# A later slot for one remainder step, matmuls on zeros before the first attention units, and decay tables computed behind the casts

## The chip, the core and the metric

The kernel runs on one core of a Trainium2 chip. The metric is the device time of the launch in microseconds (us); the median of several runs is given. The core's engines are TensorE (PE in the profile, its weight loads PEld), VectorE (DVE), ScalarE (ACT), GpSimd (POOL) and SyncE (SP). DMA is issued here from SP and from POOL.

## The reference, cut to what matters

Two stages follow each other. The first is a decayed attention without softmax over 8 batches, 8 heads, 576 positions and 64 dimensions of a head; the second is a mixture of 4 experts with given weights.

```python
scores = (1 / sqrt(64)) * (q @ k.T)                 # per batch and head, 576 x 576
D = where(i >= j, gamma[h] ** (i - j), 0)           # gamma[h] = 1 - 2 ** (-5 - h)
attn = (scores * D) @ v                             # (8, 8, 576, 64)

x = attn.transpose(0, 2, 1, 3).reshape(4608, 512)
p = probs / (probs.sum(-1) + 1e-9)                  # (4608, 4)
out = sum(p[:, e] * (relu(x @ w1[e]) @ w2[e]) for e in range(4))   # w1 512x1024, w2 1024x512
```

## The kernel before, in words

The decay is split: keys are multiplied by a table `gk` that grows with their position, and the results by a table `gq` that falls with the query's position, so that only a triangular 0/1 mask stays between them. Attention is done in chunks of 128 positions. Inside a chunk scores are masked and multiplied with v; earlier chunks come in as a running sum of k times v (`sbd`). A batch has 576 positions, four chunks and a remainder of 64 positions, which the class `Rem` handles for all heads at once.

The second stage works on 9 tiles of 512 tokens. A tile goes through 4 experts: four up groups (`up_group`, 8 matmuls of 128x128 by 512 each, with the ReLU) and then, in tile 0, two down groups (`down_plain`, 16 such matmuls each). That makes 24 slots, 0 to 23. In slots 0 to 3, 6 to 9, 12 to 15 and 18 to 21 an up group runs, in the others a down group. Later tiles have another form of the down product and 30 slots.

Everything else is hung into these slots by hand. `slots` maps a slot number to a list of functions; `run(slots, n)` calls them right after the matmuls of slot n, in the order in which they were added. Each engine then executes its share in program order. So a slot number sets at the same time the place in TensorE's order, in VectorE's, in ScalarE's and in SP's queue.

Before tile 0 come the four units of batch 0 (class `Unit`; a unit is half of the four chunks for four heads). A unit's `cast` scales k on VectorE, converts q on ScalarE and v on GpSimd. Its `trans_pe` transposes k and q on TensorE and copies them out, q with ScalarE and k with VectorE. Then come `scores`, `kv` and `values`. These steps are interleaved by hand in the loop at lines 587 to 596. The result goes to the tile `xt`, the input of the up groups. The four rows of the table `gq` are computed on ScalarE ahead of all this (line 157), as is the exponential of `gk0`.

In tile 0 these steps hang in slots:

- `remainder(slots, 0, (-1, 11, 15, 16))`: in slot 11 the casts of the remainder of batch 0 and two transposes by DMA from SP (`kTr`, `qTr`, line 299); in slot 15 its scores (`sr`, line 305); in slot 16 its values (`or`, lines 311 and 313). The input `rawr` was loaded from GpSimd's queue.
- The four units of batch 1, with (cast, scores, values) at (14, 18, 19), (17, 21, 22), (21, 24, 26) and (24, 28, 30), counted on into tile 1. Their transposes (line 491) are DMAs from SP.
- `load_p(1, e, nc.sync)` in slot 17: four DMAs of 256 KB each from SP that spread the mixing weights of tile 1 over the partitions (`pB`).
- `w_sum` in slots 17 to 26: sums of weights on VectorE, for the down product of later tiles.

The weights of the experts are loaded with a conversion from GpSimd's queue (`load_w1` line 100, `load_w2` line 103), in the order w1 of expert 0, w2 of 0, w1 of 1, w2 of 1, w1 of 2, the remainder's inputs, w2 of 2, inputs of batch 1's first unit, w1 of 3, inputs of its second unit, w2 of 3. PSUM is a ring of four tiles (`ring_tile`) that all products share.

Of the kernel before, what the change touches and what calls it, by code (L numbers as in the profile page):

```python
# [10 lines left out]
BF16 = mybir.dt.bfloat16  # L11
# [12 lines left out]
def kernel(  # L24
# [10 lines left out]
    nc = tc.nc  # L35
    B, H, S, D = q.shape
    N, E = moe_domain_probs.shape
    _, Dm, F = moe_w1.shape
# [6 lines left out]
    NP = H // 2  # L45
# [20 lines left out]
    def ring_tile(name, shape, dt=FP32):  # L66
        return ring.tile(shape, dt, tag="ring", name=name)
# [11 lines left out]
    def load_rem(b, eng=nc.sync):  # L79
        for j in range(2):  # L80
            for n, src in (("k", k), ("v", v)):
                eng.dma_start(out=rawr[n][64 * j:64 * j + 64, :, j, :],  # L82
                                  in_=src[b, j:H:2, SM:S, :].rearrange("g t d -> t g d"))
        eng.dma_start(out=rawr["q"][0:R, :, :, :].rearrange("t g j d -> t (g j) d"),
                          in_=q[b, :, SM:S, :].rearrange("h t d -> t h d"))
# [13 lines left out]
    def load_w1(e):  # L99
        return nc.gpsimd.dma_start(out=w1_sb[e], in_=moe_w1[e].rearrange("(dc p) f -> p dc f", p=128))  # L100
# [7 lines left out]
    epool = early.enter_context(tc.tile_pool(name="epool", bufs=1))  # L108
# [18 lines left out]
    nc.sync.dma_start(out=prb, in_=moe_domain_probs.rearrange("(p t) e -> p t e", p=128))  # L127


    pos_0 = epool.tile([128, 2, 2], FP32)  # L130
    nc.gpsimd.iota(pos_0, pattern=[[2 * C, 2], [1, 2]], base=0, channel_multiplier=2,
                   allow_small_or_imprecise_dtypes=True)
# [20 lines left out]
    lsc = epool.tile([128, 1], FP32)  # L153
    nc.vector.memset(lsc, math.log(scale))
    gq = const.tile([128, NP, S], FP32)
    for p in range(NP):
        nc.scalar.activation(gq[:, p, :], pos_i, Exp, scale=lgp[:, p:p + 1], bias=lsc)  # L157

    tri = const.tile([128, C], BF16)
# [49 lines left out]
    def load_p(t, e, eng):  # L209
        pB[t, e] = ppool.tile([128, NT], FP32, tag="pB", name="pB")  # L210
        eng.dma_start(out=pB[t, e], in_=pd[e:e + 1, t * NT:(t + 1) * NT].to_broadcast([128, NT]))  # L211
# [369 lines left out]

    bfv0 = lambda g: {(n, hf): bf0[n][:, hf, g] for n in "kqv" for hf in range(2)}
    us = [Unit(0, hf, g, raw0[u], bfv0(g)) for u, (hf, g) in enumerate(units0)]
    us[0].cast(nc.gpsimd)
    us[0].trans_pe()
    us[1].cast(nc.gpsimd)
    for u in range(NU):
        us[u].scores()
        us[u].kv()
        if u + 1 < NU:  # L590
            us[u + 1].trans_pe()
        if u == 0:
            load_w1(0)
        if u + 2 < NU:
            us[u + 2].cast(nc.gpsimd)
        us[u].values()
# [51 lines left out]
    def remainder(slots, b, at):  # L648
        add = lambda i, f: slots.setdefault(i, []).append(f)
        x = Rem(b)  # L650
        l, c, s, o = at
        if b > 0:
            add(l, lambda: load_rem(b))
        add(c, x.cast)
        add(c, x.trans_dma)
        add(s, x.scores)
        add(o, x.values)
# [4 lines left out]

    slots = {}
    add = lambda i, f: slots.setdefault(i, []).append(f)
    remainder(slots, 0, (-1, 11, 15, 16))

    def v_cast(u):
        vs[u].cast()
        vs[u].trans_dma()
        if u == 0:  # L670
            load_v(2, nc.gpsimd)
        elif u == 2:
            load_v(3, nc.gpsimd)
        elif u == 3:
            load_pair(raw1, 2, 0)

    def v_head(u):
        vs[u].scores()
        vs[u].kv()

    for u, (c, sc, o) in enumerate(((14, 18, 19), (17, 21, 22), (21, 24 + 0, 24 + 2), (24 + 0, 24 + 4, 24 + 6))):
        add(c, lambda u=u: v_cast(u))
        add(sc, lambda u=u: v_head(u))
        add(o, lambda u=u: vs[u].values())
    add(17, lambda: [load_p(1, e, nc.sync) for e in range(E)])
    for j in range(4):
        for wi, which in enumerate((3, 1, 2, 4)):
            add((17, 19, 22, 25)[j] + wi // 2, lambda which=which, j=j: w_sum(which, 4 * j, 4 * j + 4))
# [1 line left out]
    n = 0  # L690
# [11 lines left out]
    for t in range(1, n_nt):  # L702
        slots = {i - 24: f for i, f in slots.items() if i >= 24} if t == 1 else {}
# [6 lines left out]
        add = lambda i, f: slots.setdefault(i, []).append(f)  # L710
# [12 lines left out]
        n = 0  # L723
# [43 lines left out]
```

## Time and profile before

| what | value |
|---|---|
| median of 8 runs | 559.71 us |
| lowest and highest of them | 557.65 and 562.08 us |
| the profiled execution's own time | 560.53 us |
| its span in the trace | 558.7 us |
| PE busy in the span | 538.4 us (96%) |
| DVE busy | 375.5 us (67%) |
| ACT busy | 110.8 us (20%) |
| POOL busy | 55.0 us (10%) |
| bytes moved by DMA | 64.28 MB, mean 115 GB/s |

The profile's page cuts the span into 40 slices of 14 us each and gives a digit for the busy share of each engine in a slice. A row PEclk gives the granted TensorE clock in tenths of full speed. The view of stages gives the same for any stretch of the span. The timeline lists instructions with start, duration, and in brackets how long the engine had been idle and what ended the wait. The chain of work that ended last names, from the last instruction back, what released each step. The busy time of PE contains modelled ends of matmuls, so a PE that is shown busy need not run at its peak.

### The profile page before, as it was taken

Reading aid. Unit: us, or ns where it says so; the run is one execution under the profiler, and the core shown is the slowest. Engines: PE = TensorE matmul, PEld = TensorE weight load, DVE = VectorE, ACT = ScalarE, POOL = GpSimd, SP = SyncE. Lnnn points to the kernel's source line nnn. Section 1 sums busy time; section 2 is a strip of 40 time slices with the busy share of each in tenths; the row PEclk is TensorE's granted clock in tenths of the full one; section 3 lists DMA queues with packets and bytes.
Section 4 is the critical chain, followed back from the end, with each engine's and each line's share of the span. In section 5 each row is a group of like instructions: output and inputs, shape, how many; then the busy total and the mean of one; then the engine's idle time right before and its main releaser. Section 6 shows DMA issues by size and latency. Waiting matters only on the chain.

```text
span 558.7 us, 10556 instructions
## 1 busy us (share of the span) xinstructions
PE 538.4 (96%) x4416; PEld 351.7 (63%) x4416; DVE 375.5 (67%) x550; ACT 110.8 (20%) x216; POOL 55.0 (10%) x95
## 2 busy tenths in 40 slices
PE   4999599999999999999999999999999999999996
PEld 3544245888854686468645874588447854884485
DVE  4622067988668874897389838984788567736871
ACT  5323313303211220122013201131113100000010
POOL 4613101010000000000000000000000000000000
PEclk9999899999999999999999999999999999999999
DMA  9999918557635752577145824753367131010010
GB/s 238 165 205 238 224 34 217 103 100 152 170 91 122 151 143 72 122 133 171 57 113 131 148 87 95 156 125 103 91 136 146 51 97 40 21 57 19 1 39 38
DMA packets 147454, 64.28 MB, mean 115 GB/s; under 512 B 127216, under 2 KB 137584, under 8 KB 147408
## 3 DMA queue, kind: packets, MB, share of 16 engines
q1 hardware_dynamic: 137760, 44.35, 34.9%
q0 software_dynamic: 9648, 19.27, 16.1%
q8 instruction: 34, 0.56, 0.4%
q14 instruction: 12, 0.10, 0.1%
HBM read 53.56 MB, written 9.51 MB: 113 GB/s over the span
## 4 chain that ended last, share of the span: by engine, by line
PE 92%; DMA 3%; DVE 2%; ACT 1%; issue 1%; SPq 1%; POOL 0%; POOLq 0%; DVEq 0%; ACTq 0%
PE ph L326 37%; PE pd L429 35%; PE po L359 5%; PE ph L344 5%; DMA qTr<-bfr_q 2%; PE kvp L246 2%; PE o L270 1%; PE s L259 1%; PE o L273 1%; PE kvp L525 1%; DMA rawr_q<-in_q_dram 1%; PE pt L483 1%; PE s L506 1%; ACT gq L157 1%; SPq L82 0%
## 5 line engine op out<-in xcount | busy, mean ns | idle before, releaser
L326 PE MATMUL ph<-xt,w 128*128 128x512 bf16 x1024 | 228.8, 382 | 0.0
L326 PEld LDWEIGHTS <-w 128*128 128x128 bf16 x1024 | 99.3, 99 | 115.4 <-issue 2.9
L332 DVE SCALAR_TENSOR_TENSOR h<-ph,pB 128x1024 bf16<-128x1024 f32 x112 | 136.2, 1222 | 31.9 <-PE ph L326 31.6
L429 PEld LDWEIGHTS <-h 128*128 128x128 bf16 x1024 | 98.7, 98 | 12.2
L429 PEld LDWEIGHTS <-s 128*128 128x128 bf16 x768 | 74.3, 98 | 8.9
L429 PE MATMUL pd<-wx,h 128*128 128x256 bf16 x512 | 61.2, 273 | 0.0
L429 PE MATMUL pd<-wx,s 128*128 128x256 bf16 x512 | 61.1, 273 | 0.0
L251 ACT ACTIVATE sbd<-kvp 64x256 bf16<-64x256 f32 x48 | 18.1, 378 | 111.1 <-PE kvp L246 110.8
L261 DVE TENSOR_TENSOR sT<-s,tri 128x1024 bf16<-128x1024 f32 x24 | 29.2, 1217 | 10.9 <-PE s L259 10.9
L211 POOL DMA_DIRECT2D pB<-pd x28 | 15.2, 542 | 206.9 <-DVE h L332 168.5
L455 POOL TENSOR_TENSOR ob<-v,p 128x256 f32<-128x256 f32 x16 | 11.6, 724 | 231.5 <-DVE v L452 139.0
L359 PE MATMUL po<-wx,h 128*128 128x512 bf16 x128 | 31.0, 401 | 0.0
L429 PE MATMUL pd<-t4w,h 128*128 128x256 bf16 x256 | 30.6, 273 | 0.0
L429 PE MATMUL pd<-t2w,s 128*128 128x256 bf16 x256 | 30.6, 273 | 0.0
L446 DVE TENSOR_TENSOR u<-pd,p 128x256 f32<-128x256 f32 x16 | 6.8, 422 | 35.4 <-issue 29.5
L429 PE MATMUL pd<-t3w,h 128*128 128x256 bf16 x256 | 30.6, 273 | 0.0
L344 PE MATMUL ph<-xt,w 128*128 128x256 bf16 x256 | 29.2, 273 | 0.2 <-DVE h L347 0.2
L280 DVE TENSOR_TENSOR xt<-o,gq 128x384 bf16<-128x384 f32 (+6 forms) x48 | 18.0, 416 | 16.0 <-PE o L273 16.0
L344 PEld LDWEIGHTS <-w 128*128 128x128 bf16 x256 | 24.7, 98 | 3.2
L437 ACT ACTIVATE p<-pd 128x256 f32<-128x256 f32 x16 | 6.1, 383 | 95.5 <-PE pd L429 73.8
L330 ACT ACTIVATE h<-ph 128x1024 bf16<-128x1024 f32 x16 | 16.4, 1023 | 40.6 <-PE ph L326 40.6
L408 DVE TENSOR_TENSOR h<-h 128x1024 bf16<-128x1024 bf16 x32 | 23.4, 770 | 0.0
(130 smaller groups left out, 418.5 us busy)
## 6 DMA issues: line engine op xcount, KB each, us to landing
pB<-pd POOLq DMA_DIRECT2D x28, 256.0 KB, 3.7
raw_k<-in_k_dram SPq DMA_DIRECT2D x48, 128.0 KB, 2.9
raw_q<-in_q_dram SPq DMA_DIRECT2D x48, 128.0 KB, 3.3
raw_v<-in_v_dram SPq DMA_DIRECT2D x48, 128.0 KB, 3.4
w<-in_moe_w_dram POOLq DMA_DIRECT2D x4, 1024.0 KB, 13.1
wx<-in_moe_w_dram POOLq DMA_DIRECT2D x4, 1024.0 KB, 17.2
out_dram<-oa SPq DMA_DIRECT2D x16, 256.0 KB, 2.0
out_dram<-ob SPq DMA_DIRECT2D x16, 256.0 KB, 2.0
```

Source lines behind the costliest of these rows:

```text
L211: eng.dma_start(out=pB[t, e], in_=pd[e:e + 1, t * NT:(t + 1) * NT].to_broadcast([128, NT]))
L251: nc.scalar.activation(sbd[r, self.p, :, r], kvp[r, :, :], Copy)
L261: nc.vector.tensor_tensor(self.sT[:, :, :, :].rearrange("p j c t -> p (j c) t"), s[:, :, :, :].rearrange("p j c t -> p (j c) t"), tri[:, : ...
L280: nc.vector.tensor_tensor(xt_of(t)[:, p, n0 + a - t * NT:n0 + z - t * NT], o[:, a:z], gq[:, p, a:z], op=MULT)
L326: nc.tensor.matmul(ph[:, f, :], lhsT=w1_sb[e][:, dc, fc * 128:(fc + 1) * 128], rhs=x[:, dc, :], start=(dc == 0), stop=(dc == NDC - 1))
L330: nc.scalar.activation(h[:, fk:fk + 2, :], ph, Relu)
L332: nc.vector.scalar_tensor_tensor(h[:, fk:fk + 2, :], ph, 0.0, pB[t, e][:, :].unsqueeze(1).to_broadcast([128, 2, NT]), op0=MAX, op1=MULT)
L344: nc.tensor.matmul(ph[:, f, :], lhsT=w1_sb[e][:, dc, fc * 128:(fc + 1) * 128], rhs=x[:, dc, c], start=(dc == 0), stop=(dc == NDC - 1))
L359: nc.tensor.matmul(po[:, g, :], lhsT=h[:, e * NFC + fc, ns * 128:(ns + 1) * 128], rhs=wx[e // 2][:, (e % 2) * NFC + fc, :, :].rearrange("p ...
L408: nc.vector.tensor_tensor(h[:, l, self.b], h[:, l, self.a], h[:, l, self.b], op=SUB)
L429: mm = nc.tensor.matmul(dst, lhsT=src[:, kk, tok], rhs=rhs(c), start=(start and c == 0), stop=(c == KH - 1), skip_group_check=True)
L455: nc.gpsimd.tensor_tensor(self.ob[:, HF:Dm], self.v, self.p5, op=ADD)
```

## The change

Three things change. First, the remainder of batch 0 in tile 0 is cast in slot 12 rather than 11, has its scores in slot 18 rather than 15 and its values in slot 19 rather than 16; to go with it the first unit of batch 1 has its scores in slot 19 rather than 18 and its values in slot 20 rather than 19, and the four loads of `pB` for tile 1 stand in slot 15 rather than 17. Second, eight matmuls on a tile of zeros (128x128 by 512) run on TensorE ahead of the first unit's transposes and three more behind them; the tile is filled by VectorE. Third, the rows of `gq` are no longer computed on ScalarE ahead of the first cast: rows 0 and 1 follow the first unit's `trans_pe`, rows 2 and 3 follow the first unit's `kv`. As the loop is written, that puts rows 2 and 3 ahead of the second unit's `trans_pe` in ScalarE's order.

```diff
+    zz = epool.tile([128, 512], BF16)
+    nc.vector.memset(zz, 0.0)
+
+    def warm(n):
+        w = ring_tile("w", [128, 512])
+        for _ in range(n):
+            nc.tensor.matmul(w, lhsT=zz[:, 0:128], rhs=zz, start=True, stop=True)
+
     pos_0 = epool.tile([128, 2, 2], FP32)
...
     gq = const.tile([128, NP, S], FP32)
-    for p in range(NP):
+
+    def make_gq(p):
         nc.scalar.activation(gq[:, p, :], pos_i, Exp, scale=lgp[:, p:p + 1], bias=lsc)
...
+    warm(8)
     us[0].cast(nc.gpsimd)
     us[0].trans_pe()
+    warm(3)
+    make_gq(0)
+    make_gq(1)
     us[1].cast(nc.gpsimd)
     for u in range(NU):
         us[u].scores()
         us[u].kv()
+        if u == 0:
+            make_gq(2)
+            make_gq(3)
         if u + 1 < NU:
             us[u + 1].trans_pe()
...
-    remainder(slots, 0, (-1, 11, 15, 16))
+    remainder(slots, 0, (-1, 12, 18, 19))
...
-    for u, (c, sc, o) in enumerate(((14, 18, 19), (17, 21, 22), (21, 24 + 0, 24 + 2), (24 + 0, 24 + 4, 24 + 6))):
+    for u, (c, sc, o) in enumerate(((14, 19, 20), (17, 21, 22), (21, 24 + 0, 24 + 2), (24 + 0, 24 + 4, 24 + 6))):
...
-    add(17, lambda: [load_p(1, e, nc.sync) for e in range(E)])
+    add(15, lambda: [load_p(1, e, nc.sync) for e in range(E)])
```

## The prediction

> **What bounds the kernel now.** I read the page's rows by slices first, then the stages around the slice that sticks out, then the timeline there and the chain of waits, and last the units ahead of tile 0. TensorE is at 9 everywhere but in the first slice and the last one, and in slices 3 and 4:
>
> ```profile
> PE   4999599999999999999999999999999999999996
> PEclk9999899999999999999999999999999999999999
> ```
>
> A PE digit of 5 and a clock digit of 8, both in slice 4 (56 to 70 us), mark one place where TensorE stood still and was slowed afterwards. The view of stages by 2 us (columns: PE busy, PEld, DVE, ACT, POOL, granted clock, DMA share, GB/s):
>
> ```profile
> 58.00:60.00 2.00, 2.00 (x10) 0.70 (x8) 0.00 (x0) 1.67 (x3) 0.00 (x0) 1.00 1.13 229
> 60.00:62.00 2.00, 0.02 (x1) 0.00 (x0) 0.00 (x0) 2.00 (x4) 1.49 (x2) 1.00 1.22 196
> 64.00:66.00 2.00, 0.00 (x0) 0.00 (x0) 0.00 (x0) 0.00 (x0) 0.00 (x0) 0.78 1.22 228
> 68.00:70.00 2.00, 2.00 (x6) 0.69 (x5) 0.00 (x0) 0.00 (x0) 0.00 (x0) 0.50 1.35 123
> 70.00:72.00 2.00, 2.00 (x6) 0.73 (x5) 0.00 (x0) 0.00 (x0) 0.00 (x0) 0.51 0.22 9
> 72.00:74.00 2.00, 2.00 (x17) 1.02 (x16) 0.85 (x2) 0.00 (x0) 0.00 (x0) 1.00 0.00 0
> ```
>
> No matmul runs from 60 to 66.9 us; the clock falls to half at 65.2 us (finer stages) and is back at 71.9. The DMA engines are full until 70 and empty from 71. The timeline says what TensorE waited for:
>
> ```profile
> 55.19 1.30 SPq L299 DMA_TRANSPOSE kTr<-bfr_k  x1
> 56.59 1.19 SPq L299 DMA_TRANSPOSE qTr<-bfr_q  x1
> 57.88 1.21 SPq L491 DMA_TRANSPOSE qkT<-bf_k  x1
> 59.90 2.10 SPq L491 DMA_TRANSPOSE qkT<-bf_q  x1
> ...
> 66.93 0.37 PE L305 MATMUL sr<-qTr,kTr 128*128 128x64 bf16 x4 [6.91 <-DMA qTr<-bfr_q]
> 67.12 6.00 PE L359 MATMUL po<-wx,h 128*128 128x512 bf16 x16
> 73.18 3.62 PE L359 MATMUL po<-wx,h 128*128 128x512 bf16 x16
> ```
>
> The scores of the remainder stand behind slot 15, whose matmuls end at 59.9. Their q was sent to be transposed at 56.59 and landed 10.2 us later, at 66.8, though 2.3 us is the median for this transfer. The next 16 matmuls took 6.00 us, the 16 after them 3.62.
>
> The second place is ahead of tile 0:
>
> ```profile
> 2.80 3.14 ACT L157 ACTIVATE gq<-pos_i,lsc,lgp 128x576 f32<-128x576 f32 x4 [0.48 <-DVE lsc L154]
> 5.85 0.61 ACT L471 ACTIVATE bf_q<-raw_0q 128x512 bf16<-128x512 f32 x1
> 8.67 0.63 ACT L471 ACTIVATE bf_q<-raw_1q 128x512 bf16<-128x512 f32 x1 [0.91 <-DMA raw_1q<-in_q_dram]
> 11.87 0.64 PE L506 MATMUL s<-qkT 64*64 64x128 bf16 x16 [0.25 <-DVE qkT L486]
> 23.12 9.27 PE L326 MATMUL ph<-xt,w 128*128 128x512 bf16 x32
> 39.14 7.07 PE L326 MATMUL ph<-xt,w 128*128 128x512 bf16 x32
> ```
>
> The first 32 matmuls of tile 0 take 9.27 us and the same 32 of expert 1 take 7.07. The starts lie 0.43 us apart until 27.7 us and 0.21 to 0.22 after it. So TensorE runs at half speed up to 27.7 us, and the units too (16 score matmuls take 0.64 us here, 0.42 at 78.46), although the granted clock is printed as 1.00: there is no record before the first change.
>
> **Part 1, the slots.** A run of 16 full matmuls costs 3.45 us at full clock (the pieces of the chain), an up group half of that.
>
> Removed: the wait from 59.83 to 66.93, 7.1 us, and the slow stretch behind it, 6.0 - 3.45 = 2.5 us. Sum 9.6.
>
> Is the wait gone, or moved? The cast needs slot 11's last use of VectorE (bfr_k at 54.48), which slot 12 does not shift, since the up group of slot 12 gives VectorE nothing. bfr_q goes behind slot 12's ReLU on ScalarE (54.88 + 1.02) and ends at 56.5; SP is ready for qTr at 56.59 because kTr holds it until then. So both transposes leave at their old times and land at 64.0 and 66.8. The scores now stand behind slots 16, 17 and 18: 59.83 + 6.9 + 1.73 = 68.5. The margin is 1.7 us.
>
> What is late next is VectorE: after slot 17 (66.75) come two accumulations (1.41), the key cast of unit 1 (0.68) and two weight sums (1.4) ahead of the remainder's mask: 70.4, then 0.42. TensorE, done with slot 19 at 70.4, waits for it until 70.85: 0.45 us. Behind it stands unit 0's head. Its transposes landed at 70.7 and 71.1 and it comes up at 71.1. I charge nothing, but there is no margin here. The reads of sbd in the remainder's values stay ahead of unit 0's writes, since both are in slot 19 in that order.
>
> The four loads of pB are moved past unit 1's two transposes on SP. They follow unit 0's transposes at about 61.2 us, SP being held by them until then, and no longer leave at 81.5. In the stages from 83 to 87 us they filled 0.55 + 1.00 + 0.87 + 0.36 = 2.8 us of the DMA engines. These were empty from 71 us on, so the backlog would end near 74. Unit 1's transposes leave at 69 and 70.3, behind it, and are needed at 76.2. The last weights (issued at 51.0, 16.9 us to land, 67.9) are needed at 77. GpSimd's queue keeps its order. Cost 0, between 0 and 2 us.
>
> Part 1 gives 9.6 - 0.45 = 9.1 us.
>
> **Part 2, gq on ScalarE.** One row is 3.14 / 4 = 0.79 us. The first cast of q moves from 5.85 to 4.75, where its data lands (issued 1.31, 3.4 to land), and the first scores from 8.27 to 7.1. That is not kept: the second unit's cast waits for data at 8.67 in any case. In ScalarE's order then come bf_q to 9.3, two copies to sbd (0.77) to 10.07, the two rows of gq (1.57) to 11.64, the copy of the transposed q (0.60), VectorE's copy of k (0.42), and so the scores at 12.8 where they were at 11.87. Cost 0.9 us, as long as what follows is bounded by TensorE. Rows 0 and 1 lie in a gap (6.7 to 8.27) and cost nothing.
>
> **Part 3, the zeros.** The fill of VectorE runs while it waits for pos (idle to 1.10). Eight matmuls at 0.427 us run from about 1.1 to 4.5; the transposes come at 4.65, so nothing waits. Three more (1.28) lie under the copies of the transposed tiles, from 5.85 to 7.13; the scores come at 7.1. So the direct cost is 0. PSUM's ring gains two tiles without readers.
>
> What they bring depends on the clock. The rows: dense matmuls from 23.12 changed it at 27.7, after 4.6 us; from 66.93 at 71.9, after 5.0; it fell at 65.2, some 5.3 us after the last. The units, shown 95% busy from 10 to 20 us, never changed it. The nearest row asks for 4.6 us of dense matmuls; the change gives 3.4, then 1.3 more, with transposes and waits between. And it would have to last: between 10.2 and 12.8 us TensorE has nothing, and the first weights, landing at 19.6, keep the up groups from starting earlier.
>
> The Trainium skill (TensorE: Matmul & The Clock Gate, Part 1) says that the clock is raised after one busy window of about 3.4 us, and that windows run freely. My trace agrees: 65.2 to 71.9 is two windows of 3.4, of which the first, half filled, changed nothing. By this rule eight matmuls fill a window only if its phase fits or if a part suffices. Part 4 of the page speaks against the change: transposes do not count as busy in the same way; no run here shows that. By the rows and Part 4 the units stay slow: gain 0, the front end ends 0.9 us later. If the clock is raised and holds: scores of unit 1 at 12.8; unit 1 takes 3.3 us (scores and kv at full speed 1.31, sbd 0.87, copies 1.08); unit 2 takes 3.1 (VectorE: 0.68 + 0.77 + 1.21 + 0.43); unit 3 takes 2.5; tile 0 starts at 21.7 where it was 23.1, gain 1.4, and its first 32 matmuls take 6.91 and not 9.07, gain 2.2. Ends: -0.9 and +3.6. I take -0.9, by the nearest row.
>
> **Sum.** 9.1 - 0.9 = 8.2 us. The profiled execution took 560.5 (span 558.7 and 1.8 around it), 0.8 above the median, and its two slow stretches (4.6 and 5.0 us) are of ordinary length. So I take the sum from the median: 559.7 - 8.2 = 551.5.
>
> **The rivals.**
>
> A, the forecast: the wait gone, the units slow. 551.5; with 0 to 1.5 us of new waits up to 553. Chance 0.47.
>
> B, the clock raised and held: 9.1 + 3.6 = 12.7 gained, less what DMA takes back: TensorE then wants unit 1's transposes at 72.6, with pB's loads ahead of them until about 74, 0 to 1.5 us. 547.0 to 548.5. For it: 4.7 us of added matmuls. Against: gaps and small matmuls. 0.33.
>
> C, part of the wait stays: every transfer under load took 8.8 to 12.8 us, and margins of 1.7 and 0 us are thin. With 3 us waited in slot 18 or 19: 554.5; 553 to 557. 0.12.
>
> D, slower: the wait moves to unit 0's head in slot 19, as pB's 1 MB and the last weights hold its transposes. It decides from a landing at about 77: 6 us of wait, and the clock lost again (2.5), outweigh 8.2. At 79: 562. For it: 57.88 to 70.7 was already 12.8 us. Against: the loads of pB are issued behind these transposes, and the DMA engines run empty at 71. 0.08.
>
> **How the numbers follow.** A measurement of this kernel can tell about 0.5%, 2.8 us, from no change. Faster by more: A, B and three quarters of C, 0.89; within: the rest of C and 0.01 of D, 0.04; slower: 0.07. The range 546.5 to 555.0 holds A, B and the lower half of C.
>
> **What would show it.** Right: no PE idle over 1 us between slot 15 and slot 18, `sr` at about 68 to 69 us, clock 1.00 from 56 to 74, unit 1's first scores near 12.8, the first ph group at 0.43 us spacing. B shows in a first ph group of about 7 us. Wrong: an idle PE ahead of `sr`, or ahead of unit 0's scores behind slot 19, with a DMA of qTr or qkT as the releaser.

## The result, and the profile after

| | before | changed |
|---|---|---|
| median | 559.67 us (32 executions, 557.16 to 562.21) | 554.96 us (11 executions, 552.44 to 558.79) |
| ratio of times, 95% interval | | 0.992 (0.9897 to 0.9942) |
| profiled execution, its span | 560.53 us, 558.7 us | 553.99 us, 552.1 us |

The change gains 4.7 us by the medians, 3.2 to 5.8 by the interval. (A ratio and its interval leave out executions more than 1.5% above the fastest of their kernel.) The record holds a twelfth execution of the changed kernel, 551.32 us, which is not in this median; with it the median would be 554.7. The forecast was a gain of 8.2. The direction was right, and the size is little more than half of it. "Granted clock" of an execution means below the mean over its span, 1 being full speed.

The page of the changed kernel, busy tenths in 40 slices of 13.8 us. The 5 and the 8 of slice 4 are gone; a 5 has come to PEclk in slice 1, ahead of tile 0:

```profile
PE   6999999999999999999999999999999999999996
PEclk9599999999999999999999999999999999999999
```

The timeline of the changed kernel at the place of the old wait. Lines of the later file are shifted by 9 to 16, so L308 and L314 are the transposes and scores of the remainder, L500 unit 0's transposes and L515 its scores:

```profile
57.72 1.19 SPq L308 DMA_TRANSPOSE qTr<-bfr_q  x1
61.03 1.96 SPq L500 DMA_TRANSPOSE qkT<-bf_q  x1
...
60.99 7.29 PE L368 MATMUL po<-wx,h 128*128 128x512 bf16 x32
69.84 0.28 PE L314 MATMUL sr<-qTr,kTr 128*128 128x64 bf16 x4
72.36 0.42 PE L515 MATMUL s<-qkT 64*64 64x128 bf16 x16
77.43 0.42 PE L515 MATMUL s<-qkT 64*64 64x128 bf16 x16
```

The timeline of before has unit 1's scores, the last of these lines, here:

```profile
85.39 0.42 PE L506 MATMUL s<-qkT 64*64 64x128 bf16 x16
```

The remainder's scores wait for nothing that the profile shows. The down groups that took 6.00 + 3.62 us take 7.29. Unit 1's scores come at 77.43 where they came at 85.39: 8.0 us gained at this point, in this execution. At the end of the span 6.6 are left, since three waits for a landing in later tiles (0.7, 0.2 and 0.5 us) are not in the profile of before. Such waits come and go: over the profiles of the runs below, but for the one with later heads, the time from unit 1's scores to the end of the span lies between 472.6 and 475.7 us (before: 473.3, changed: 474.7).

Ahead of tile 0:

```profile
1.26 3.59 PE L136 MATMUL w<-zz 128*128 128x512 bf16 x8 [1.26 <-DVE zz L131]
10.22 1.62 ACT L166 ACTIVATE gq<-pos_i,lsc,lgp 128x576 f32<-128x576 f32 x2
11.87 0.60 ACT L494 ACTIVATE qkT<-pt 128x512 bf16<-128x512 bf16 x1
12.98 0.64 PE L515 MATMUL s<-qkT 64*64 64x128 bf16 x16 [2.42 <-ACT bf_q L480]
24.24 9.29 PE L335 MATMUL ph<-xt,w 128*128 128x512 bf16 x32
```

Two rows of gq stand between sbd and the copy of q on ScalarE, TensorE is idle for 2.4 us, unit 1's scores come at 12.98 where they came at 11.87, and tile 0 starts at 24.24 where it started at 23.12. The clock was raised at 4.8 us and fell again at 11.6, so that tile 0's first matmuls take 9.29 us as before.

This one execution does nearly what the forecast said. It is 1 us below the median of its kernel, and the profiled execution of before is 0.9 us above its own; the experiments ask what the others do.

### The profile page after: what moved, and what is told of

It reads as the page before. It is cut to its first block, busy times and chain, and to the rows that moved or that the text cites. A ratio compares the mean times of both kernels' runs of the same rounds, so it can differ in the third digit from the quotient of the medians.

```text
span 552.1 us, 10579 instructions
## 1 busy us (share of the span) xinstructions
PE 539.2 (98%) x4427; PEld 351.5 (64%) x4427; DVE 375.6 (68%) x551; ACT 110.4 (20%) x216; POOL 55.0 (10%) x95
## 4 chain that ended last, share of the span: by engine, by line
PE 86%; DMA 5%; DVE 3%; SPq 2%; ACT 1%; issue 1%; POOL 0%; POOLq 0%; ACTq 0%; DVEq 0%
PE pd L438 34%; PE ph L335 34%; PE ph L353 5%; PE po L368 5%; PE kvp L255 2%; DMA qTr<-bfr_q 1%; PE s L268 1%; PE o L279 1%; PE kvp L534 1%; DMA raw_1q<-in_q_dram 1%; DMA rawr_q<-in_q_dram 1%; SPq L82 1%; PE o L282 1%; DMA raw_v<-in_v_dram 1%; DMA qkT<-bf_q 1%
## 5 line engine op out<-in xcount | busy, mean ns | idle before, releaser
L464 POOL TENSOR_TENSOR ob<-v,p 128x256 f32<-128x256 f32 x16 | 11.6, 724 | 232.5 <-DVE v L461 139.4
L368 PE MATMUL po<-wx,h 128*128 128x512 bf16 x128 | 28.6, 379 | 0.0
L378 DVE SCALAR_TENSOR_TENSOR acc<-po,pm,acc 128x512 f32<-128x512 f32 x12 | 8.5, 747 | 23.9 <-PE po L368 23.9
```

The lines of the kernel that those rows point to most:

```text
L368: nc.tensor.matmul(po[:, g, :], lhsT=h[:, e * NFC + fc, ns * 128:(ns + 1) * 128], rhs=wx[e // 2][:, (e % 2) * NFC + fc, :, :].rearrange("p ...
L464: nc.gpsimd.tensor_tensor(self.ob[:, HF:Dm], self.v, self.p5, op=ADD)
```

## The experiments

The theory at the start: the slots gain what was worked out, and the front end takes 1 us back. The rivals: a transpose still lands late in many executions; or the front end costs far more.

**The parts alone.** Later slots (and pB's loads in slot 15) in the kernel before:

```diff
-    remainder(slots, 0, (-1, 11, 15, 16))
+    remainder(slots, 0, (-1, 12, 18, 19))
-    for u, (c, sc, o) in enumerate(((14, 18, 19), (17, 21, 22), ...
+    for u, (c, sc, o) in enumerate(((14, 19, 20), (17, 21, 22), ...
-    add(17, lambda: [load_p(1, e, nc.sync) for e in range(E)])
+    add(15, lambda: [load_p(1, e, nc.sync) for e in range(E)])
```

> The kernel before with the later slots alone (remainder at 12, 18, 19, unit 0 of batch 1 at 19 and 20, the loads of pB in slot 15); gq and TensorE's start as before. Theory 1 (the slots are worth what was worked out, the front end takes about 1 us of it back): 9 us faster than before, 550 to 551. Theory 2 (the margins are thin, so that in most executions a transpose still lands late in slot 18 or 19): 5 to 6 us faster, 554. Theory 3 (the front end costs much more than the trace of one execution shows): 11 us faster or more, below 549.

Measured: 552.00 us beside 559.38, ratio 0.9884 (0.9847 to 0.9921). Its profiled execution, 551.09, has unit 1's scores at 76.20: 9.2 us earlier than before. That is theory 1 as far as the profile goes. But its six executions run from 550.6 to 556.2, and the two slowest have the lowest granted clocks (0.996 and 0.994, the others 0.998 to 1.000).

The opposite, the changed kernel with these three lines put back:

> The changed kernel with the slots and the loads of pB put back: zeros and the moved rows of gq alone. Theory 1: 1 us slower than before (0.5 to 1.5), 560.7, with the first matmul of tile 0 at about 24.2 us where it was 23.1, and the wait for the remainder's transposes as before. Theory 2: the same. Theory 3: 3 us slower or more.

Measured: 560.91 beside 559.38, ratio 1.0025 (1.0010 to 1.0041), so 1.4 us slower (0.6 to 2.3). Tile 0 starts at 24.3, and the remainder's wait is still there (4.4 us). The front end takes back what was expected; theory 3 falls.

Without the zeros:

```diff
-    warm(8)
...
-    warm(3)
```

> The changed kernel without the eleven matmuls on zeros; slots and gq as changed. If the zeros bring nothing (the clock falls again before tile 0): same as the changed kernel, 555 within 0.5. If in a part of the executions the clock holds through the units: 1 to 2 us slower than the changed kernel. If the zeros do harm: faster.

Measured: 554.32, ratio 0.9905 (0.9872 to 0.9938), which is not told apart from the changed kernel. No value of the zeros is seen here. What matters is how its eight executions divide: three at 550.9 to 552.2 us have a granted clock of 0.999, five at 554.1 to 558.5 have 0.993 to 0.997. In this kernel there is no record of a low clock ahead of tile 0, so the low clock of those five must lie elsewhere. The timeline of its profiled execution (554.06) says where:

```profile
58.98 1.36 SPq L500 DMA_TRANSPOSE qkT<-bf_q  x1
72.14 0.42 PE L515 MATMUL s<-qkT 64*64 64x128 bf16 x16 [1.76 <-DMA qkT<-bf_q]
73.16 3.45 PE L335 MATMUL ph<-xt,w 128*128 128x512 bf16 x8
77.01 1.24 PE L335 MATMUL ph<-xt,w 128*128 128x512 bf16 x5
```

Unit 0's scores in slot 19 wait 1.76 us for the unit's own transpose, and the 8 matmuls of slot 20 take 3.45 us, not 1.89. The stages (behind each stretch first its length, then the busy time of PE, PEld, DVE, ACT and POOL, granted clock, DMA share, GB/s):

```profile
68.00:70.00 2.00, 1.81 (x12) 0.70 (x9) 1.97 (x5) 1.18 (x2) 0.00 (x0) 1.00 0.81 82
70.00:72.00 2.00, 0.38 (x8) 0.26 (x7) 1.56 (x3) 0.86 (x1) 0.00 (x0) 1.00 0.95 251
72.00:74.00 2.00, 1.86 (x35) 1.15 (x36) 1.39 (x2) 0.72 (x2) 0.00 (x0) 0.73 1.55 318
74.00:76.00 2.00, 2.00 (x6) 0.74 (x5) 1.12 (x2) 0.04 (x1) 0.00 (x0) 0.50 0.72 182
```

The clock falls at 72.9 us and is back at 76.3. So the old picture is here again in small: a wait for a transpose, then a slow stretch. It is not in the changed kernel's profile, because that execution started tile 0 later: TensorE came to slot 19's scores at 72.3, when the transpose had landed at 72.2.

Rows 2 and 3 of gq later:

```diff
-        if u == 0:
+        if u == 1:      # moved behind us[u + 2].cast(nc.gpsimd)
             make_gq(2)
             make_gq(3)
```

> The changed kernel with rows 2 and 3 of gq computed behind the cast of the fourth unit (so behind the transposes of the third) and no longer ahead of the second unit's transposed copy. Theory 1: the second unit's scores come at 11.2 to 11.9 us and not at 13.0; 1 us faster than the changed kernel, 554, with the clock still falling before tile 0. If the empty stretch of TensorE from 10.5 to 13.0 us was what lost the clock, it now holds and the first 32 matmuls of tile 0 take 7 us: 3 to 5 us faster than the changed kernel, 550 to 552. Theory 2: no change in time, since the transposes in tile 0 set it.

Measured: 557.14 for the median of all six executions, 548.3 to 558.4. The ratio, 0.9877 (0.9820 to 0.9934), rests on the three fastest (548.3, 552.7 and 556.4) and says little. The profiled one (558.00) came to slot 19's scores at 70.1 us, waited there and ran slow behind it:

```profile
73.80 0.64 PE L515 MATMUL s<-qkT 64*64 64x128 bf16 x16 [3.66 <-DMA qkT<-bf_q]
75.22 3.59 PE L335 MATMUL ph<-xt,w 128*128 128x512 bf16 x8
```

A TensorE that comes earlier finds the same transfer still under way, gives its gain back, and loses the clock on top. One execution, 548.33 at a clock of 0.997, shows what is there to be had.

**The loads of pB.** Slot 17 again, in the changed kernel and with the slots alone:

> The changed kernel with the four loads of pB put back into slot 17, behind the second unit's transposes on SP; all else as changed. Theory A (these loads, 1 MB in the same queue and on the same DMA engines, keep the first unit's transposes, so that TensorE waits in slot 19 and loses the clock in a part of the executions): the transposes land by 70 us, no wait for them ahead of unit 0's scores, 2 to 3 us faster than the changed kernel, 552 to 553, with a narrow spread. Theory B (the transposes land at 71 to 74 us in any case, as the weights fill the DMA engines until then): same as the changed kernel, 554 to 555.

> The kernel before with the later slots of the remainder and of unit 0's head, and nothing else: the loads of pB stay in slot 17, gq and TensorE's start as before. Theory A: 9 us faster than before, 550.3, and all executions within 3 us, none with a wait for unit 0's transposes. Theory B: as slots alone with pB in slot 15 (552.0), with executions up to 556.

Measured: 552.89 (0.9884, 0.9844 to 0.9924), with four executions at 552.1 to 553.1 and two at 556.7 and 558.1; and 556.57 (0.9914, 0.9877 to 0.9952), with two at 550.6 and 551.1 (clock 0.999 and 0.998) and five at 556.0 to 557.1 (0.993 to 0.995). Theory A asked for a narrow spread in both. It falls: with the loads of pB out of the way there are still executions 4 to 6 us above the others, with a lower clock. That these wait in slot 19 is inferred from their clock, since the two profiled executions (552.46 and 550.55) are among the lower ones and have no wait there. Whether the loads cost something is not settled.

**What keeps the transposes.** Unit 2's loads were to leave later:

```diff
-        if u == 0:
-            load_v(2, nc.gpsimd)
...
+    add(18, lambda: load_v(2, nc.gpsimd))
```

> The changed kernel with the three loads of batch 1's third unit (0.75 MB, GpSimd's queue) issued in slot 18 and not in slot 14; they are needed in slot 21. Theory B (unit 0's transposes land when the DMA engines have worked off what is queued, at 70 to 74 us, whenever they are issued): with 0.75 MB less ahead they land 2 to 3 us earlier, by 69 us in the profile; the wait in slot 19 is gone, the clock stays up from tile 0 to the end, 552 to 553 with no execution above 555. If the transposes' own time is what holds them (13 us each way under load): as the changed kernel, 555.

Measured: 557.03 (0.9926, 0.9885 to 0.9966), seven executions from 552.3 to 561.8. The edit did not do what it says: in the trace these loads leave at 56.2, 60.3 and 61.0 us, where the changed kernel has 57.2, 61.3 and 62.0. On GpSimd's queue their issue waits for VectorE and ScalarE to have read the buffers (releasers bf_k and bf_q in the timeline), not for TensorE, so a later slot holds nothing there. The run says nothing on either theory; it is in effect the changed kernel once more. From SP's queue, where unit 1's transposes stand ahead, the place holds:

```diff
+    add(18, lambda: load_v(2, nc.sync))
```

> The changed kernel with the third unit's loads (0.75 MB) in slot 18 from SP's queue, behind the second unit's transposes, so that they cannot leave before about 70 us (from GpSimd's queue the place in the program did not hold them: they left at 56 to 61 as before). Theory B (the DMA engines' backlog sets the landing of unit 0's transposes): they land 2 to 3 us earlier, by 69 to 70 us, fewer executions with a wait, median 552 to 553. If the backlog that counts is that of the weights alone: as the changed kernel, 555.

Measured: 552.23 (0.9876, 0.9852 to 0.9900), with the loads at 73 to 74 us, five executions from 551.3 to 553.3 and one at 555.3. This is what theory B asked for. The landing in the profiled execution, the view of DMA issues (KB where given, us to landing), first of the changed kernel, then of this one:

```profile
qkT<-bf_q SPq DMA_TRANSPOSE x1, 11.2
```

```profile
qkT<-bf_q SPq DMA_TRANSPOSE x1, 8.2
```

From 61.03 to 72.2 and from 60.59 to 68.8. That points to the backlog. One landing proves little, though: in the run above, with the old backlog, it was 69.4, and in one below (clock held in slot 19) 67.0. The profiled execution here is the one at 555.3; it has neither a wait in slot 19 nor a low clock behind it, and takes 2.4 us more than before from unit 1's scores to the end. Over the profiles that bear on it ("ready" is when TensorE had done all that stands ahead of unit 0's scores):

| profile | sent | landed | TensorE ready | wait | low clock behind |
|---|---|---|---|---|---|
| changed | 61.0 | 72.2 | 72.3 | 0 | none |
| slots alone, pB in 17 | 58.8 | 69.7 | 70.1 | 0 | none |
| unit 2's loads moved, without effect | 60.0 | 69.4 | 71.3 | 0 | none |
| clock held in slot 19 (below) | 60.4 | 67.0 | 71.6 | 0 | none |
| no zeros | 59.0 | 72.0 | 70.4 | 1.8 | 3.4 us |
| gq rows later | 58.7 | 73.6 | 70.1 | 3.7 | 6.8 us |
| clock held ahead of tile 0 (below) | 55.5 | 70.2 | 66.9 | 3.5 | 6.8 us |
| the same, unit 2's loads moved (below) | 55.0 | 68.8 | 66.4 | 2.5 | 6.8 us |
| the same, unit 0's head in slot 20 (below) | 56.2 | 72.9 | 69.3 | 3.7 | 6.8 us |

The landing lies at 67 to 74 us, and TensorE is ready at 66 to 72, depending on the front end. Sent at 55 to 56 us, with the clock held ahead of tile 0, the transfer lands at 69 to 73, hardly earlier than where it is sent at 59 to 61.

**The heads later.** A unit's head is its scores and its kv. Those of units 0 and 1 in slots 21 and 22:

> The changed kernel with the heads of batch 1's first two units later: scores of unit 0 in slot 21 and of unit 1 in slot 22 (values in 22 and 23) where they were in 19 and 21; pB's loads stay in slot 15. Both theories say that the wait in slot 19 costs the difference: no wait for qkT, clock at 1.00 from 30 us to the end, 552 to 553; up to 1 us may come back at the start of tile 1, where unit 1's values are late. If the wait in slot 19 is not what costs: 555 as the changed kernel or slower.

Measured: 553.30 (0.9877, 0.9847 to 0.9907), 552.5 to 555.5; the profiled one (555.45) has its clock at 1.00 behind 27.4 us and waits 1.1 us for xt at the start of tile 1. The upper end of the changed kernel (558.8) is gone and the median is 1.7 us lower, near the 552 to 553 that both theories gave, although the intervals of the two kernels overlap.

**The clock held.** Ten matmuls on weights ahead of unit 0's scores, in the changed kernel and with the slots alone:

```diff
             s = ring_tile("s0", [128, 2, 2, 2, C])
+            for _ in range(held):
+                nc.tensor.matmul(s[:, 0].rearrange("p g r t -> p (g r t)"), lhsT=w1_sb[0][:, 0, 0:128],
+                                 rhs=w1_sb[0][:, 0, 0:512], start=True, stop=True)
```

> The changed kernel with ten matmuls of 128x128 by 512 on weights ahead of unit 0's scores in slot 19, into the scores' own tile (overwritten by the scores): they keep TensorE at work while it waits for the transposes and change nothing of the wait. If the lost clock is a large part of the cost: no execution with the clock at half behind tile 0's start, the slow executions (557 to 559) are gone, median 553 to 554, although up to 2.2 us of matmuls are added where there was no wait. If the wait alone costs: 555 to 557.

> The kernel before with the later slots alone (pB's loads in slot 17), and ten matmuls on weights ahead of unit 0's scores in slot 19, overwritten by the scores. Without them this kernel had executions at 551 and at 556 to 557. If the upper ones are a wait and a lost clock: none above 554, all within 2 us, median 551.5 to 552.5 (the matmuls cost up to 2.2 us where there was no wait). If the upper ones have another cause: executions at 556 stay.

Measured for the first: 554.02 (0.9898, 0.9875 to 0.9921), as expected, all six executions from 553.5 to 554.6. In its profile, whose transposes landed at 67.0:

```profile
71.65 2.32 PE L510 MATMUL s<-w 128*128 128x512 bf16 x10
73.90 0.42 PE L518 MATMUL s<-qkT 64*64 64x128 bf16 x16
```

The ten matmuls took 2.3 us, and the slowest execution is 4 us below the slowest of the changed kernel (558.8). For the second: 555.02 (0.9924, 0.9902 to 0.9947), 554.0 to 557.3, a miss by 3 us. Hardly any clock was lost (0.997 and above), yet executions at 556 and 557 stay. The profiled one, 555.01, waits 2.8 us for transposes in later tiles (2.4 us at the remainder's scores, 0.4 at unit 2's); the profile of the same kernel without the ten matmuls, 550.55, has 1.0. So a part of the spread arises behind slot 19. Where the executions at 556 and 557 lose their time was not profiled and stays open.

The clock held ahead of tile 0 (pB's loads in slot 17, the rows of gq late):

```diff
-        us[u].scores()
+        us[u].scores(3 if u else 0)      # so many matmuls on zeros into the scores' tile first
```

> The changed kernel with pB's loads in slot 17, rows 2 and 3 of gq behind the fourth unit's cast, and three more matmuls on zeros ahead of the scores of each of units 1, 2 and 3, in the scores' own tile (they are overwritten by the scores). If zeros in the gaps keep the clock up to tile 0: its first 32 matmuls take about 7 us and not 9, the units are bounded by VectorE and ScalarE, tile 0 starts at 20 to 21.5 us: 546 to 549. If the clock falls in spite of them: 4 us slower than that, 551 to 553, as the zeros then cost 0.4 us each.

Measured: 552.62 (0.9852, 0.9816 to 0.9887), 550.1 to 555.1. That misses the 546 to 549 expected if the clock holds, though ahead of tile 0 it does hold: in the profile it stays up from 5 us to 69.8, and tile 0 runs at full speed from its start. The gain is lost in slot 19:

```profile
21.25 6.75 PE L335 MATMUL ph<-xt,w 128*128 128x512 bf16 x30 [0.33 <-DVE xt L582]
70.39 0.64 PE L518 MATMUL s<-qkT 64*64 64x128 bf16 x16 [3.48 <-DMA qkT<-bf_q]
78.19 0.42 PE L518 MATMUL s<-qkT 64*64 64x128 bf16 x16
```

TensorE is 5.5 us ahead of the changed kernel at the remainder's scores (64.3 and 69.8) and 0.8 us behind it at unit 1's (78.19 and 77.43).

Two attempts to mend this, the first with the edit of unit 2's loads that does nothing from GpSimd's queue, the second with unit 0's head in slot 20 besides:

> The kernel with the clock held ahead of tile 0 (zeros ahead of each unit's scores, late rows of gq, pB's loads in slot 17), and the third unit's loads in slot 18. Theory B: TensorE arrives at unit 0's head at 67 us; the transposes land at 67 to 69, a wait of 0 to 2 us remains and the clock holds in most executions: 548 to 550. If the loads are not what keeps the transposes: 552.6 as without this edit.

> As the run before this one, with unit 0's scores in slot 20 and its values in slot 21 where they were in 19 and 20. Theory B: the last of the wait goes too, the clock holds to the end of every execution, 547 to 548. If it is slower than the run before, the later head costs more at unit 1's head (slot 21) than the wait did.

Measured: 553.30 (0.9880, 0.9847 to 0.9914) and 550.35 (0.9830, 0.9791 to 0.9868). Both are slower than theory B asked for (548 to 550 and 547 to 548). The second has executions at 547.1 and 547.7 with a clock of 1.000, and up to 553.4 where it waits 3.7 us and loses the clock.

**The transfer taken away.** Units 0 and 1 of batch 1 are transposed on TensorE, so that slot 19 has no DMA to wait for:

```diff
-    ident = epool.tile([128, 128], BF16)
+    ident = t4w[:, KH - 1, 0:128]
...
-        vs[u].trans_dma()
+        if u > 1:
+            vs[u].trans_dma()
...
+    add(16, lambda: vs[0].trans_pe())
+    add(20, lambda: vs[1].trans_pe())
```

In the changed kernel, and in the kernel with the clock held ahead of tile 0:

> The changed kernel with batch 1's first two units transposed on TensorE (in slots 16 and 20, eight matmuls each, copied out by ScalarE and VectorE) and not by DMA: the wait in slot 19 has nothing left to wait for. Cost: 16 transposes of 56 ns, 0.9 us, and two copies each. If that wait and the clock lost behind it are what the forecast lacked: no execution above 555, the clock up from tile 0 on, median 552.5 to 553.5. If not: 555 to 556, with the spread of the changed kernel.

> The same transposes on TensorE in the kernel with the clock held ahead of tile 0 (zeros ahead of each unit's scores, late rows of gq, pB's loads in slot 17). If the wait in slot 19 was what ate the front end's gain of 5 us: 546 to 548, all executions within 3 us. If another transfer (the last weights, landing at 68) takes its place: 549 to 551, with TensorE waiting ahead of slot 18 or 22.

Measured: 552.28 (0.9867, 0.9845 to 0.9888), all four executions from 551.6 to 552.6; and 549.11 (0.9815, 0.9793 to 0.9837), all five from 548.8 to 550.1. In the profile of the first, eight transposes take 0.45 us (63.36 to 63.81; the line below has four of them) and unit 0's scores wait for nothing:

```profile
63.36 0.39 PE L492 MATMUL pt<-t4w,bf_k 128*128 128x128 bf16 x4
71.51 0.42 PE L515 MATMUL s<-qkT 64*64 64x128 bf16 x16
```

The granted clock is 0.986 to 0.987 in all executions of the first, which is what the slow stretch ahead of tile 0 makes of it, and 0.999 to 1.000 in all of the second: no clock is lost in slot 19. The interval of the first (0.9845 to 0.9888) lies clear of that of the changed kernel (0.9897 to 0.9942). The second kernel has the lowest median of the study with a narrow spread, 10.7 us below before and 5.8 below the changed one by the medians; it misses its 546 to 548 by 1 us. Its stages around slot 19, in the columns of above:

```profile
62.00:66.00 4.00, 4.00 (x24) 1.87 (x23) 2.96 (x5) 1.02 (x1) 0.00 (x0) 1.00 1.07 336
66.00:70.00 4.00, 3.81 (x56) 2.24 (x55) 3.96 (x7) 1.83 (x4) 0.00 (x0) 1.00 0.27 93
70.00:74.00 4.00, 4.00 (x68) 2.27 (x66) 3.24 (x8) 2.77 (x4) 0.00 (x0) 1.00 0.02 6
```

PE is busy for 3.81 us of 4 or more and the clock is whole. VectorE is busy for 3.96 of 4 in the second stretch; that it is the next limit is not shown. This profile has 2.6 us of waits for transposes of later units and tiles, against 0.6 in the profile of the first kernel, which is enough for the missing 1 us.

The front end without that wait in the way: the old front end with these slots and transposes, and the changed one with the two rows of gq late:

> The kernel before with the later slots, pB's loads in slot 15 and batch 1's first two units transposed on TensorE; gq and TensorE's start as before. Against the same with the changed front end (552.3, all within 1 us) it shows what the front end costs without the wait of slot 19 in the way. As forecast: 0.9 us, so 551.4. If the front end costs more (the profile of the front end alone showed the first scores of unit 1 later by 1.1 us): 551.0 or less. If it costs nothing: 552.3.

> The changed kernel with the first two units of batch 1 transposed on TensorE and rows 2 and 3 of gq behind the fourth unit's cast. If the two rows ahead of the second unit's copy are what the front end costs: 1 to 2 us faster than without this edit (552.3), 550.5 to 551.3. If in some executions the clock now holds through the units: these at 548 to 549.

Measured: 551.18 (0.9868, 0.9841 to 0.9895) and 549.51 (0.9832, 0.9805 to 0.9859). By the medians the changed front end (552.28) costs 1.1 us; by the ratios, 0.9867 and 0.9868, nothing; so few runs do not tell 0.9 from 0. The later rows of gq gain 2.0 us by the ratios, at the upper end of the 1 to 2 expected. In the profiled execution (548.21) the clock held from 6.1 to 19.7 us and was back at 23.2.

## Why the prediction was right or wrong

- *The removed wait and slow stretch, 9.6 less 0.45.* Right. The slots alone gain 9.2 us at unit 1's scores against 9.1, in an execution without a wait. The small wait for VectorE was 0.2 us, not 0.45, in the changed kernel.
- *The remainder's transposes land at 66.8, margin 1.7 us.* Right in most profiles (66.9 in the changed kernel, where its scores come at 69.84); one shows a wait of 0.6 us there.
- *gq, 0.9 us lost.* Right in mechanism and about in size: 1.1 in the trace, 1.4 (0.6 to 2.3) for the front end alone; 0 to 1.1 with the transfer of slot 19 taken away.
- *The zeros: units stay slow, value -0.9 for the front end.* Right in outcome, for half of the reason. I held that the clock would not be raised, since dense matmuls had needed 4.6 us for it; here 3.6 us raised it at 4.8. It then fell at 11.6, inside the stretch in which I had TensorE empty (10.2 to 12.8; measured 10.6 to 13.0). By the Trainium skill (TensorE: Matmul & The Clock Gate, Part 1) windows last 3413 ns and run freely. The trace agrees: the raised stretch (4.82 to 11.64, 6.83 us) is two of them, the slow one behind it (17.07 us) five.
- *"Behind it stands unit 0's head ... I charge nothing, but there is no margin here."* This is the step that failed: the wait for unit 0's transposes and the clock behind it were charged at nothing, because one landing (71.1) was set against one arrival (71.1). In the runs the landing scatters from 67 to 74 us and the arrival from 66 to 72. Where TensorE comes first, the profiles show a wait of 1.8 to 3.7 us and then 3.4 to 6.8 us at half clock, which cost 1.7 to 3.4 more. Without these transfers the changed kernel is at 552.28 instead of 554.96. That is 2.7 us, and it carries 0.9 us of new transposes (twice the 0.45 us of the trace), so it accounts for about the missing 3.5 us. Later heads, with the transfers kept, point the same way (553.30), and with ten matmuls in the place of the wait no execution is above 554.6.

  No trace of the changed kernel itself shows the wait; its profiled execution has none. Its times and clocks allow an estimate: taking half of the time at half clock off each of the twelve spans leaves 540.8 to 546.1 us, with 13 to 23 us at half clock; without the transfers it leaves 542.8 to 543.2, with 14 to 15. In the mean each part costs 1.2 us less, the first in spite of the 0.9 us of transposes, so the waits cost no less than the clock. How much of it are waits in later tiles is not separated. What decides an execution's arrival was not tested; in the profiles TensorE is ready later where the clock came back later at the start of tile 0 (two profiles with the slots alone: back at 25.3 us and ready at 70.1, back at 27.0 and ready at 71.1; the changed kernel: 28.7 and 72.3).
- *Rival D, "It decides from a landing at about 77: 6 us of wait, and the clock lost again".* The place and the mechanism were right, as a way to lose part of the gain. The threshold was not: I took from the trace of before that about 5.3 us without a matmul are needed. A wait of 1.76 us was enough, with only light work around it (four pairs of small matmuls ahead, unit 0's scores behind). In size it is rival C, "part of the wait stays", that came true, at 0.12. Worked out with the clock's price in it, at a wait of 2 us (551.5 + 2 + 1.7), it would have stood at 555, where the kernel is.
- *Rival B, DMA takes back 0 to 1.5 us.* Too little: in the profile with the clock held the whole 5.5 us were lost in slot 19.
- *pB's loads, 0 to 2 us.* Not settled by the runs.

## What to carry to other kernels

Moving a step away from a late transfer moves TensorE to the next one: list the landings that the same backlog sets and compare each with the new arrival time, not with the old one. A place with no margin has a price even where one profile shows no wait: take the wait that the landing's scatter allows and add the half clock behind it. A kernel whose executions spread widely is read by the granted clock of each execution beside its time.

## What the runs showed of the hardware

- The clock fell after an idle stretch of 1.76 us, in a window of 3.4 us in which the profile has TensorE busy for 1.45 us (69.5 to 72.9 us in the kernel without zeros). The Trainium skill (same page, "Why this matters for your kernels") says to have no idle gaps above about 3 us between bursts; here the measurement decides, and it asks for less. The filled share alone does not decide it: 1.72 us of dense matmuls in 3.4 (58.3 to 61.7 us of before) kept the clock, 1.75 us of small ones (8.2 to 11.6 us of the changed kernel) lost it. No threshold is shown.
- Matmuls on zeros count for the clock. Eight of them raised it (at 4.8 us in the changed kernel). Three (about 0.65 us at full clock) ahead of each later unit's scores kept it up to tile 0 in all four profiles that have them; with the same rows of gq and without them it fell at 8.7 us in one profile and at 19.7 in another.
- A transposing DMA of one unit took 6.4 to 16.7 us to land when it was sent at 55 to 61 us, among the other loads, against a median of 2.5 over the span. Sent at 55 to 56 us it landed at 69 to 73, sent at 59 to 61 at 67 to 74.
